# Symmetric attention scores: half of the diagonal chunk of query groups 1 to 4, its place in the program, and a trip through DRAM for its corners

## The chip, the cores and the metric

One core of one Trainium2 chip runs the program. The time is the device time of one execution in microseconds (us). A profiled execution gives the trace that is quoted here; its engines are called PE (TensorE matmuls), PEld (TensorE weight loads), DVE (VectorE), ACT (ScalarE), POOL (GpSimd) and SP (SyncE, which only issues transfers here).

## The reference

```python
scores = (1 / S) * np.matmul(z, z.transpose(0, 2, 1))   # B = 8, S = 3072, 64 wide
attn = np.maximum(scores, 0.0) ** 2
x = u * np.matmul(attn, v)                              # 256 wide
...
x = _moe_ref(x, ...)      # 8 experts, top 1, 256 -> 1024 -> 256
return _moe2_ref(x, ...)  # max of three products, then one more
```

`z` meets itself, so the score matrix of a batch is symmetric, and so is its rectified square.

## The kernel before, in words

The program has three stages: attention over 8 batches, the experts, and a last dense layer. The change is in the first.

A batch's 3072 rows are cut into 6 chunks of 512. A **group** is one batch `b` and one chunk `q` of queries; there are 48, in the order of batches and then of `q` from 0 to 5. A **unit** is one group and one block `kb` of 128 keys; a group has 24 units, four for each chunk `c` of keys. `unit(t)` turns a running number into group, batch, chunk and key block.

fp32 products are made of fp32r parts, a high and a low one. For a unit, `scores(t)` makes a tile `s` of 128 keys x 512 queries with two matmuls of 512 columns (L265 with `hh`, L266 with `ll`; the weights are the key block of `hl`). `square(t, s)` rectifies it on ACT into `a` (L271) and squares it on ACT (L274) or on DVE (L277), whichever is less ahead by a running count of nanoseconds (`hold`, `ahead`). `split_a(t)` makes the high part `ahi` on ACT (L299) and the low part `alo` on DVE (L300). `attend(t)` multiplies them with the values: four times a matmul of 512 columns (L332) and one of 256 (L333).

Symmetry is used between chunks already. For key chunks behind the query chunk (`c > q`) DVE also turns the tile in 32x32 blocks (L306, `turned`), and each finished chunk, 1 MB, is stored to DRAM (`mirror`, L310). When group `c` comes to key chunk `q`, it does not compute: `fetch_back` has read the chunk into a tile `back` (four transfers, L318), and `split_a` reads that. Such units are called **mirrored**; group `q` has 4q of them, at its start. There are three `back` tiles in a ring, so that a fetch waits until the chunk of three fetches ago is used up (`done` in the loop over `pairs`).

The order of the program is written out by hand as a loop over steps `t`. In step `t`, `split_a` is called for unit t+3 (`AH` is 3), `scores` and `square` for unit t+5 unless it is mirrored, and `attend` for unit t. What is scheduled with `at(t, ...)` comes first in its step. `step()` runs pieces of background jobs in between: loading `z` and `v`, the end of a group (`arrive`), the routing for the experts (`route`), and `weights`, which converts the last layer's weights in 48 parts of twelve DVE instructions (`split_m2`, on tiles `wex`, `wsg`, `wmt`, `wrs`, `fr`, `both`). A piece is put off where DVE or ACT is counted too far ahead. What is left of `weights` after the attention is run behind the first block of the experts (`for _ in weights: pass`); there DVE also makes a table of block addresses (`lims`, `tab`), from which SP reads where to fetch the rows of the third block (`wgs<-xb`).

## Time and profile before

| | |
|---|---|
| median of 3 runs | 4076.74 us (4076.67 to 4077.44) |
| the profiled execution, its own time | 4076.14 us |
| its span, first to last instruction | 4074.1 us |
| mean granted TensorE clock, share of full | 0.998 |
| PE busy, PEld busy | 4032.8 us (99%), 3441.0 us (84%) |
| DVE busy, ACT busy, POOL busy | 3151.4 us (77%), 2411.1 us (59%), 1143.9 us (28%) |
| last matmul of the attention starts | 2005.03 us |

The span is what the trace shows; 2 us of the execution's time lie around it. Busy time of PE contains modelled ends of matmuls, so the distance between the starts of matmuls says more than their durations.

### The profile page before, as it was taken

To read this page: it belongs to the slowest core of one execution; us is meant where nothing else is said; L and a number is where in the kernel's file an instruction comes from. 1 tells how busy PE (TensorE), PEld (TensorE's weight loads), DVE (VectorE), ACT (ScalarE), POOL (GpSimd) and SP (SyncE) were. 2 spreads that over 40 slices of the span, in tenths; PEclk is the share of its full clock that TensorE was granted. 3 is DMA by queue.
4 is the path that set the end of the run, shared out by engine and by line. 5 is a ranking of instruction groups with operands and counts; after the bars stand their busy time and mean duration, and the time that the engine had idled before them with its cause. 6 is when DMAs were issued, how large, how long until landed. Compare 5 with 4: busy or idle time off the path is not lost. (4 is left out here: it accounts for less than half of the span.)

```text
span 4074.1 us, 62853 instructions
## 1 busy us (share of the span) xinstructions
PE 4032.8 (99%) x21156; PEld 3441.0 (84%) x21156; DVE 3151.4 (77%) x5925; ACT 2411.1 (59%) x4419; POOL 1143.9 (28%) x1228
## 2 busy tenths in 40 slices
PE   9999999999999999999999999999999999999999
PEld 7888888888888888888899999888888888888887
DVE  8888888888888888888755555677777777777776
ACT  8777787877868778687533333344444444444443
POOL 0111111112111121111321121255455455455453
PEclk9999999999999999999999999999999999999999
DMA  6877868677786777958654554412211221221211
GB/s 179 193 191 194 186 189 196 177 192 175 198 205 164 198 193 195 202 163 196 153 144 129 130 139 121 102 31 32 42 33 31 42 34 29 42 36 27 42 32 21
DMA packets 880303, 507.14 MB, mean 124 GB/s; under 512 B 518050, under 2 KB 831522, under 8 KB 864578
## 3 DMA queue, kind: packets, MB, share of 16 engines
q1 hardware_dynamic: 856946, 438.04, 46.3%
q0 software_dynamic: 20880, 64.28, 5.2%
q8 instruction: 175, 2.87, 0.3%
q14 instruction: 190, 1.56, 0.1%
q10 hardware_dynamic: 2112, 0.39, 0.1%
HBM read 277.62 MB, written 200.31 MB: 117 GB/s over the span
## 5 line engine op out<-in xcount | busy, mean ns | idle before, releaser
L332 PE MATMUL acc<-vt,ahi 128*128 128x512 f32 x4608 | 1647.2, 396 | 4.5 <-DVE x L349 2.4
L333 PE MATMUL acc<-vt,alo 128*128 128x256 f32 x4608 | 1291.4, 280 | 3.9 <-DVE alo L300 3.9
L1253 PE MATMUL ph<-mx,mw 128*128 128x512 f32 x4536 | 1196.9, 395 | 6.3 <-POOL mx L668 3.9
L332 PEld LDWEIGHTS acc<-vt,ahi 128*128 128x128 f32 x4608 | 866.0, 188 | 210.6 <-DVE x L349 4.3
L1253 PEld LDWEIGHTS ph<-mx,mw 128*128 128x128 f32 x4536 | 850.7, 188 | 213.2 <-POOL mx L668 14.1
L333 PEld LDWEIGHTS acc<-vt,alo 128*128 128x128 f32 x4608 | 870.6, 189 | 34.5 <-DVE alo L300 5.4
L1259 ACT ACTIVATE spare<-ph 128x512 f32<-128x512 f32 x648 | 384.6, 597 | 645.2 <-PE ph L1253 641.0
L300 DVE TENSOR_TENSOR alo<-a,ahi 128x512 fp32r<-128x512 f32 x672 | 465.6, 693 | 171.1 <-ACT ahi L299 163.5
L112 POOL DMA_INDIRECT xb<-x,idx x192 | 223.7, 1165 | 1332.4 <-DVE x L349 1058.5
L1290 PE MATMUL y<-fh,mo 128*128 128x512 f32 x1728 | 536.1, 392 | 0.3 <-DVE fh L668 0.3
L271 ACT ACTIVATE a<-s 128x512 f32<-128x512 f32 x672 | 398.6, 593 | 166.9 <-PE s L266 132.4
L668 POOL TENSOR_TENSOR fh<-fc,fh 128x512 fp32r<-128x512 f32 x285 | 367.1, 1295 | 415.2 <-ACT fh L667 399.0
L299 ACT ACTIVATE ahi<-a 128x512 fp32r<-128x512 f32 x672 | 411.6, 618 | 0.9 <-DVE a L277 0.9
L299 ACT ACTIVATE ahi<-back 128x512 fp32r<-128x512 f32 x480 | 291.5, 627 | 165.4 <-PE acc L332 125.9
L1290 PEld LDWEIGHTS y<-fh,mo 128*128 128x128 f32 x1728 | 324.7, 188 | 75.1 <-DVE fh L668 0.6
L300 DVE TENSOR_TENSOR alo<-back,ahi 128x512 fp32r<-128x512 f32 x480 | 328.7, 690 | 38.9 <-ACT ahi L299 28.5
L306 DVE STREAM_TRANSPOSE turned<-a 128x512 f32<-128x512 f32 x480 | 337.7, 704 | 0.0
L274 ACT ACTIVATE a<-a 128x512 f32<-128x512 f32 x496 | 314.0, 633 | 15.8
L694 ACT ACTIVATE h_hi<-ph 128x512 fp32r<-128x512 f32 (+1 forms) x232 | 125.4, 546 | 264.2 <-PE ph L690 235.6
L265 PE MATMUL s<-hh,hl 128*128 128x512 f32 x672 | 269.4, 401 | 9.5 <-DVE hl L201 7.1
L266 PE MATMUL s<-ll,hl 128*128 128x512 f32 x672 | 266.3, 396 | 0.0
L695 DVE SCALAR_TENSOR_TENSOR h_lo<-ph,h_hi 128x512 fp32r<-128x512 f32 (+1 forms) x232 | 144.5, 628 | 156.0 <-ACT h_hi L694 116.8
(169 smaller groups left out, 5321.8 us busy)
## 6 DMA issues: line engine op xcount, KB each, us to landing
mirror<-turned SPq DMA_DIRECT2D x120, 1024.0 KB
back<-mirror SPq DMA_DIRECT2D x480, 256.0 KB
ut<-in_u SPq DMA_DIRECT2D x48, 512.0 KB
out<-xr SPq DMA_DIRECT2D x188, 128.0 KB
vr<-in_v POOLq DMA_DIRECT2D x46, 512.0 KB
xq<-xb SPq DMA_DIRECT2D x320, 64.0 KB
r<-in_moe_w SPq DMA_DIRECT2D x16, 1024.0 KB
wgs<-xb SPq DMA_DIRECT2D x192, 64.0 KB
```

Of the source, the lines that this page charges most:

```text
L265: nc.tensor.matmul(s, w, hh, start=True, stop=False)
L271: nc.scalar.activation(a, s, AF.Relu)
L274: nc.scalar.activation(a, a, AF.Square)
L299: nc.scalar.activation(hi, a, AF.Copy)
L300: nc.vector.tensor_tensor(lo, a, hi.bitcast(F32), op=ALU.subtract)
L306: nc.vector.transpose(out=turned[0][:, :, n], in_=a.rearrange("k (c j) -> k c j", j=Q))
L332: nc.tensor.matmul(o, hn, vv, start=kb == 0, stop=False, skip_group_check=True)
L333: nc.tensor.matmul(o[:, 0], ln, vv[:, 0], start=False, stop=kb == KB - 1, skip_group_check=True)
L668: eng.tensor_tensor(lo, src, hi.bitcast(F32), op=ALU.subtract)
L1253: nc.tensor.matmul(bank[:, 0:e.n], lt[:, s, c], rt[:, m], start=start and k == 0, stop=k == 2, skip_group_check=True)
L1259: nc.scalar.activation(t, bank[:, 0:e.n], AF.Copy)
L1290: nc.tensor.matmul(flat[2 * t + d][:, 0:p.n], mo[f][:, s, d], p.h[g, i, t][m], start=(g, i, k) == (0, 0, 0), stop=(g, i, k) == (NG2 - 1, 1 ...
```

## The change

In groups with `q` from 1 to 4 (`half`) the diagonal key chunk (`c == q`) is moved to the end of the group (`order`) and treated as a mirrored one. Its scores are made earlier, by `diagonal(g, n)`, in steps in which a mirrored unit makes none. Key block n computes only the queries from block n on: 512, 384, 256 and 128 columns for n = 0 to 3. The squares go into a `back` tile. The blocks below the diagonal are turned by DVE in 32x32 blocks into `tips` (3, 2, 1 and 0 transposes), stored to DRAM (`store_corner`, four transfers) and read back into the same tile (`fetch_corner`, three transfers). The `back` ring now serves these tiles as well, so the steps at which chunks are fetched are computed anew.

```diff
@@ -231,10 +231,13 @@
         NG = B * QG
         NU = NG * KB
 
+        half = [0 < q < QG - 1 for q in range(QG)]
+        order = [[c for c in range(QG) if c != q or not half[q]] + [q] * half[q] for q in range(QG)]
+
         def unit(t):
-            g, kb = divmod(t, KB)
+            g, i = divmod(t, KB)
             b, q = divmod(g, QG)
-            return g, b, q, kb
+            return g, b, q, order[q][i // TB] * TB + i % TB
 
         a_t = {}
         back = {}
@@ -243,6 +246,12 @@
             (p, c, q): dpool.tile([P, TB * T], F32, name=f"mirror{p}_{c}_{q}")
             for p in range(2) for q in range(QG) for c in range(q)
         }
+        TX = TB * (TB - 1) // 2 * Q
+        corner = {
+            (p, q): dpool.tile([P, TB * TX], F32, name=f"corner{p}_{q}")
+            for p in range(2) for q in range(QG) if half[q]
+        }
+        tips = {}
         hi_t = {}
         lo_t = {}
         acc = {}
@@ -282,7 +291,57 @@
 
         def mirrored(t):
             _, _, q, kb = unit(t)
-            return kb // TB < q
+            return kb // TB < q or kb // TB == q and half[q]
+
+        def back_tile():
+            back_n[0] += 1
+            return slab("back") if back_n[0] % 3 else back_p.tile([P, TB, TB, P], F32, name="back")
+
+        back_n = [-1]
+
+        def tip_of(n):
+            return slice(n * (n - 1) // 2 * Q, n * (n + 1) // 2 * Q)
+
+        def diagonal(g, n):
+
+            b, q = divmod(g, QG)
+            finish_job(("z", (b, q)))
+            hold("pe", 427 * (TB - n) // TB)
+            hh, ll = zq[g]
+            w, cols = hl[b, q][:, n * P:(n + 1) * P], slice(n * P, T)
+            s, a = bank_tile("s", [P, T]), slab("a")
+            nc.tensor.matmul(s[:, cols], w, hh[:, cols], start=True, stop=False)
+            nc.tensor.matmul(s[:, cols], w, ll[:, cols], start=False, stop=True)
+            nc.scalar.activation(a[:, cols], s[:, cols], AF.Relu)
+            hold("act", 500 * (TB - n) // TB)
+            if n == 0:
+                back[b, q, q] = back_tile()
+                tips[g] = slab("turned", [P, TB, TX], name="tips")
+            x = a[:, cols].rearrange("j (k p i) -> j p k i", p=TB, i=Q)
+            o = back[b, q, q][:, n].rearrange("j p (k i) -> j p k i", i=Q)[:, :, n:]
+            if ahead("act") <= ahead("dve"):
+                nc.scalar.activation(o, x, AF.Square)
+                hold("act", 530 * (TB - n) // TB)
+            else:
+                nc.vector.tensor_tensor(o, x, x, op=ALU.mult)
+                hold("dve", 600 * (TB - n) // TB)
+            for m in range(n + 1, TB):
+                tip = tips[g][:, :, tip_of(m)][:, :, n * Q:(n + 1) * Q]
+                nc.vector.transpose(out=tip, in_=back[b, q, q][:, n, :, m * Q:(m + 1) * Q])
+                hold("dve", 240)
+
+        def store_corner(g):
+            b, q = divmod(g, QG)
+            dst = corner[b % 2, q].rearrange("(p j) (c x) -> p j c x", j=Q, c=TB)
+            for p in range(TB):
+                nc.sync.dma_start(dst[p].rearrange("j c x -> c j x"), tips[g][:, p])
+            tips.pop(g)
+
+        def fetch_corner(g):
+            b, q = divmod(g, QG)
+            src = corner[b % 2, q].rearrange("k (c x) -> k c x", c=TB)
+            for n in range(1, TB):
+                nc.sync.dma_start(back[b, q, q][:, n, :, 0:n * Q], src[:, :, tip_of(n)])
 
         def split_a(t):
             g, b, q, kb = unit(t)
@@ -299,7 +358,7 @@
             nc.scalar.activation(hi, a, AF.Copy)
             nc.vector.tensor_tensor(lo, a, hi.bitcast(F32), op=ALU.subtract)
             hold("act", 520)
-            hold("dve", 600 if c <= q else 1200)
+            hold("dve", 600 if mirrored(t) else 1200)
             if c > q:
                 if n == 0:
                     turned[0] = slab("turned")
@@ -311,8 +370,8 @@
                         mirror[b % 2, q, c], turned[0].rearrange("k c n i -> k (c n i)")
                     )
 
-        def fetch_back(n, b, c, q):
-            back[b, c, q] = t = slab("back") if n % 3 else back_p.tile([P, TB, TB, P], F32, name="back")
+        def fetch_back(b, c, q):
+            back[b, c, q] = t = back_tile()
             src = mirror[b % 2, c, q].rearrange("(p j) (n m x) -> m j n p x", j=Q, m=TB, x=P)
             for m in range(TB):
                 nc.sync.dma_start(t[m * Q:(m + 1) * Q], src[m])
@@ -320,17 +379,18 @@
         def attend(t):
             g, b, q, kb = unit(t)
             hold("pe", 1280)
-            if kb == 0:
+            i = t % KB
+            if i == 0:
                 acc[g] = [None] * TB
             hi, lo = hi_t.pop(t), lo_t.pop(t)
             vv = vt[b, kb // TB][:, kb % TB]
             for n in range(TB):
-                if kb == 0:
+                if i == 0:
                     acc[g][n] = bank_tile("acc", [P, 2, D])
                 o = acc[g][n]
                 hn, ln = hi[:, n * P:(n + 1) * P], lo[:, n * P:(n + 1) * P]
-                nc.tensor.matmul(o, hn, vv, start=kb == 0, stop=False, skip_group_check=True)
-                nc.tensor.matmul(o[:, 0], ln, vv[:, 0], start=False, stop=kb == KB - 1, skip_group_check=True)
+                nc.tensor.matmul(o, hn, vv, start=i == 0, stop=False, skip_group_check=True)
+                nc.tensor.matmul(o[:, 0], ln, vv[:, 0], start=False, stop=i == KB - 1, skip_group_check=True)
 
         xhi = xs_p.tile([P, 2 * TB, D], F32R, name="xhi")
         xlo = xs_p.tile([P, 2 * TB, D], F32R, name="xlo")
@@ -618,13 +678,28 @@
                 at(t0, start, ("v", key), prep_v(*key))
             if b or c:
                 at((b * QG + c) * KB - 12, spread_z, b * QG + c)
-        pairs = [(b, c, q) for b in range(B) for q in range(QG) for c in range(q)]
-        done = []
-        for n, (b, c, q) in enumerate(pairs):
-            t0 = b * G + q * KB + c * TB
-            made = b * G + c * KB + (q + 1) * TB - AH
-            at(max(made, done[n - 3] if n >= 3 else 0, t0 - 24), fetch_back, n, b, c, q)
-            done.append(t0 + TB - AH)
+        done = [-99] * 3
+        taken = -99
+        halved = {}
+        for g in range(NG):
+            b, q = divmod(g, QG)
+            for c in range(q):
+                t0 = g * KB + c * TB
+                made = b * G + c * KB + (order[c].index(q) + 1) * TB - AH
+                assert taken <= max(made, done[-3], t0 - 24)
+                taken = max(made, done[-3], t0 - 24)
+                at(taken, fetch_back, b, c, q)
+                done.append(t0 + TB - AH)
+            if half[q]:
+                t0 = g * KB + max(TB * q - 10 - (q == 2), -AH - 2)
+                assert t0 >= max(taken, done[-3])
+                taken = t0
+                for n in range(TB):
+                    assert mirrored(t0 + n + AH + 2)
+                    halved[t0 + n] = g, n
+                at(t0 + TB, store_corner, g)
+                at(t0 + TB + 2, fetch_corner, g)
+                done.append(g * KB + KB - AH)
         at(KB // 2, load_u, 0)
         for g in range(NG):
             e0 = (g + 1) * KB
@@ -837,6 +912,8 @@
                 ready(t + AH + 2)
                 if not mirrored(t + AH + 2):
                     square(t + AH + 2, scores(t + AH + 2))
+                elif t in halved:
+                    diagonal(*halved.pop(t))
                 step()
             if 0 <= t + 2 < NU:
                 _, b, _, kb = unit(t + 2)
```

Three places in the order of instructions follow, without times. On PE, the first diagonal chunk of the program (batch 0, group 1): before, the first score pair of the chunk, the attend matmuls of one unit (`acc<-vt,...`) and the next pair; then the same of the change.

```order
L265 MATMUL s_737<-hh_527,hl_196 128x512
L266 MATMUL s_737<-ll_528,hl_196 128x512
L332 MATMUL acc_268<-vt_654,ahi_695 128x512
L333 MATMUL acc_268<-vt_654,alo_696 128x256
L332 MATMUL acc_271<-vt_654,ahi_695 128x512
L333 MATMUL acc_271<-vt_654,alo_696 128x256
L332 MATMUL acc_274<-vt_654,ahi_695 128x512
L333 MATMUL acc_274<-vt_654,alo_696 128x256
L332 MATMUL acc_277<-vt_654,ahi_695 128x512
L333 MATMUL acc_277<-vt_654,alo_696 128x256
L265 MATMUL s_772<-hh_527,hl_196 128x512
L266 MATMUL s_772<-ll_528,hl_196 128x512
```

```order
L313 MATMUL s_691<-hh_535,hl_204 128x512
L314 MATMUL s_691<-ll_536,hl_204 128x512
L392 MATMUL acc_276<-vt_516,ahi_622 128x512
L393 MATMUL acc_276<-vt_516,alo_623 128x256
L392 MATMUL acc_279<-vt_516,ahi_622 128x512
L393 MATMUL acc_279<-vt_516,alo_623 128x256
L392 MATMUL acc_282<-vt_516,ahi_622 128x512
L393 MATMUL acc_282<-vt_516,alo_623 128x256
L392 MATMUL acc_285<-vt_516,ahi_622 128x512
L393 MATMUL acc_285<-vt_516,alo_623 128x256
L313 MATMUL s_720<-hh_535,hl_204 128x384
L314 MATMUL s_720<-ll_536,hl_204 128x384
```

The second pair has 384 columns instead of 512, and the pairs stand four attend units earlier than before, between mirrored units.

On DVE, after the first block of the experts (`xr<-y,xr` ends that block; `h_lo<-ph,h_hi` is the low part of a hidden tile that PE multiplies next): before, the address table begins at once.

```order
L723 SCALAR_TENSOR_TENSOR xr<-y,xr 128x256 x4
L891 TENSOR_TENSOR lims<-runs,base 128x8
L892 TENSOR_SCALAR lims<-lims 128x1
L894 CAST tab<-lims 1x8
L896 TENSOR_SCALAR last<-lims 1x8
L898 TENSOR_SCALAR two<-lims 1x8
L904 TENSOR_TENSOR xT<-thr,last 1x8x6
L905 TENSOR_TENSOR xT<-thr,two 1x8x43
L906 TENSOR_SCALAR xT<-two 1x8
L695 SCALAR_TENSOR_TENSOR h_lo<-ph,h_hi 128x512
```

With the change, conversion of the last layer's weights (`wex`, `wsg`, `wmt`, `wrs`, `fr`, `both`) stands there; 22 such instructions come before `lims`.

```order
L798 SCALAR_TENSOR_TENSOR xr<-y,xr 128x256 x4
L547 TENSOR_SCALAR wex<-wex 128x128
L549 TENSOR_SCALAR wsg<-w_24518 128x128
L551 SCALAR_TENSOR_TENSOR wsg<-wex,wsg 128x128
L553 TENSOR_SCALAR wmt<-w_24518 128x128
L555 SCALAR_TENSOR_TENSOR wmt<-w_24518,wmt 128x128
L770 SCALAR_TENSOR_TENSOR h_lo<-ph,h_hi 128x512
L557 TENSOR_TENSOR wmt<-wmt,wsg 128x128
L559 TENSOR_SCALAR wrs<-w_24518 128x128
L743 TENSOR_TENSOR w<-r_24246,w 128x512
L564 SCALAR_TENSOR_TENSOR fr<-wrs,wsg 128x128
L566 TENSOR_TENSOR wmt<-wmt,both 128x128
```

The table is then finished (`tab<-nblk`) right ahead of the transpose `xt<-wgs`, which reads rows that SP fetches by that table; before, 15 instructions stood between the two, now three.

```order
L992 TENSOR_REDUCE nblk<-xT 1x8
L770 SCALAR_TENSOR_TENSOR h_lo<-ph,h_hi 128x512
L993 CAST tab<-nblk 1x8
L103 TENSOR_TENSOR away<-tok_65,lims 128x36
L104 SCALAR_TENSOR_TENSOR own<-away 128x36
L105 SCALAR_TENSOR_TENSOR away<-away,tokN 128x36
L748 STREAM_TRANSPOSE xt<-wgs 128x384
L743 TENSOR_TENSOR xT<-xt,xT 128x384
L770 SCALAR_TENSOR_TENSOR h_lo<-ph,h_hi 128x512
```

On SP, group 4 of batch 0: before, the fetch of a mirrored chunk (`back<-mirror_0_5`) is followed by weight parts and the next fetch.

```order
L318 DMA back<-mirror_3_4_126 32x16x128 x4
L229 DMA ut<-in_u 128x4x256
L318 DMA back<-mirror_0_5_127 32x16x128 x4
L509 DMA mwd_75<-both 256x1x128
L460 DMA w_2500<-in_moe_w 128x256
L318 DMA back<-mirror_1_5_128 32x16x128 x4
L222 DMA hh<-hl 64x512 x2
L222 DMA ll<-hl 64x512 x2
L318 DMA back<-mirror_2_5_129 32x16x128 x4
```

With the change the corner is stored right behind it, and the next fetch (`back<-mirror_1_5`) stands behind the three reads of the corner.

```order
L377 DMA back<-mirror_3_4_126 32x16x128 x4
L229 DMA ut<-in_u 128x4x256
L377 DMA back<-mirror_0_5_127 32x16x128 x4
L337 DMA corner_4_150<-tips 4x32x192 x4
L222 DMA hh<-hl 64x512 x2
L222 DMA ll<-hl 64x512 x2
L344 DMA back<-corner_4_150 128x4x32
L344 DMA back<-corner_4_150 128x4x64
L344 DMA back<-corner_4_150 128x4x96
L377 DMA back<-mirror_1_5_128 32x16x128 x4
L569 DMA mwd_75<-both 256x1x128
L520 DMA w_2678<-in_moe_w 128x256
```

The four issues of the store, the spread of `z` (`hh`, `ll`) and the three reads now stand between two fetches of mirrored chunks.

## Rows read from the trace of the kernel before

**Rows 1.** One window of 250 us; busy us per engine, PEclk, DMA share, GB/s.
```profile
500.00:750.00 250.00, 249.61 (x1389) 215.58 (x1388) 214.39 (x476) 193.81 (x358) 38.60 (x60) 1.00 0.75 188
```

**Rows 2.** The longest waits of PE, 20 to 2000 us; total, times, longest.
```profile
PE acc L332 <- DVE x L349: 2.4, 6, 0.4
PE acc L332 <- ACT ahi L299: 2.2, 2, 1.7
```

**Rows 3.** Timeline of PE; start, us, instruction.
```profile
403.29 0.39 PE L265 MATMUL s<-hh,hl 128*128 128x512 f32 x1
403.52 0.39 PE L266 MATMUL s<-ll,hl 128*128 128x512 f32 x1
403.75 0.28 PE L378 MATMUL pm<-xhi,wgs 128*128 128x256 f32 x1
...
404.70 0.39 PE L332 MATMUL acc<-vt,ahi 128*128 128x512 f32 x1
```

**Rows 4.** Timeline of PE in the experts, 384 columns.
```profile
2052.21 3.29 PE L690 MATMUL ph<-xT,e 128*128 128x384 f32 x18
2055.34 0.40 PE L709 MATMUL y<-e,h_hi 128*128 128x256 f32 x2
```

**Rows 5.** Groups by line and shape, DVE and ACT; busy, mean ns, idle before.
```profile
L277 DVE TENSOR_TENSOR a<-a 128x512 f32<-128x512 f32 x173 | 118.3, 684 | 32.7 <-ACT a L271 26.7 <-issue 4.9
L386 DVE STREAM_TRANSPOSE L<-pm 128x128 f32<-128x128 f32 x1 | 0.3, 307 | 0.0
L300 DVE TENSOR_TENSOR alo<-back,ahi 128x512 fp32r<-128x512 f32 x480 | 328.7, 690 | 38.9 <-ACT ahi L299 28.5 <-issue 4.4 <-PE acc L333 1.1
L274 ACT ACTIVATE a<-a 128x512 f32<-128x512 f32 x494 | 312.7, 633 | 15.8
L299 ACT ACTIVATE ahi<-back 128x512 fp32r<-128x512 f32 x480 | 291.5, 627 | 165.4 <-PE acc L332 125.9 <-issue 17.3 <-DVE alo L300 8.4
```

**Rows 6.** Windows of groups 1 and 4 of batch 2.
```profile
555.20:599.30 44.10, 44.10 (x248) 38.06 (x246) 38.26 (x93) 37.03 (x69) 0.00 (x0) 1.00 0.64 170
...
682.40:719.80 37.40, 37.40 (x210) 32.39 (x209) 32.21 (x72) 23.48 (x44) 12.51 (x20) 1.00 1.06 242
```

**Rows 7.** Weight conversion on DVE, dearest and cheapest of its twelve groups of 48.
```profile
L508 DVE TENSOR_TENSOR both<-wmt,fr 128x128 fp32r<-128x128 f32 x48 | 13.5, 281 | 0.4
...
L487 DVE TENSOR_SCALAR wex<-wex 128x128 int32<-128x128 int32 x48 | 9.5, 198 | 0.3
```

**Rows 8.** Timeline of DVE at the start of the experts; idle time before in brackets.
```profile
2035.93 0.15 DVE L916 CAST tab<-nblk 1x8 int32<-1x8 f32 x1
...
2040.27 0.69 DVE L695 SCALAR_TENSOR_TENSOR h_lo<-ph,h_hi 128x512 fp32r<-128x512 f32 x1 [0.67 <-ACT h_hi L694]
...
2043.09 0.69 DVE L695 SCALAR_TENSOR_TENSOR h_lo<-ph,h_hi 128x512 fp32r<-128x512 f32 x1 [1.46 <-issue]
2043.69 0.57 DVE L673 STREAM_TRANSPOSE xt<-wgs 128x384 f32<-128x384 f32 x1
2044.85 0.56 DVE L668 TENSOR_TENSOR xT<-xt,xT 128x384 fp32r<-128x384 f32 x1 [0.59 <-issue]
2045.97 0.69 DVE L695 SCALAR_TENSOR_TENSOR h_lo<-ph,h_hi 128x512 fp32r<-128x512 f32 x1 [0.56 <-ACT h_hi L694]
```

**Rows 9.** Timeline of SP's issues in the same stretch.
```profile
2039.19 4.11 SPq L127 DMA_DIRECT2D wgs<-xb  x8
```

**Rows 10.** Timeline of PE at the attention's end; idle before in brackets.
```profile
1993.55 0.50 PE L332 MATMUL acc<-vt,ahi 128*128 128x512 f32 x1 [1.67 <-ACT ahi L299]
...
2000.92 0.56 PE L333 MATMUL acc<-vt,alo 128*128 128x256 f32 x1 [3.71 <-DVE alo L300]
```

**Rows 11.** Windows behind these two waits.
```profile
1994.20:1997.50 3.30, 2.93 (x8) 2.13 (x8) 3.30 (x3) 1.44 (x4) 3.27 (x3) 0.50 1.10 279
2000.90:2004.30 3.40, 3.38 (x11) 2.90 (x12) 0.56 (x1) 0.18 (x1) 0.05 (x1) 0.51 0.00 0
```

**Rows 12.** Waits of SP's queue from 400 to 2000 us.
```profile
SPq L318 <- DMA mirror<-turned: 67.2, 18, 5.2
```

2 lines of the change are left out of this document (1 added, 1 removed).

## The prediction

> **What bounds it now.** I read the attention first, in windows of 250 us: PE is busy for 249.6 of 250 us at the full clock, DVE for 214, ACT for 194, and the DMA engines for 0.75 of the time [rows 1]. Since PE's busy time has modelled ends, I then asked for its waits: the largest two from 20 to 2000 us sum to 4.6 us, in a stretch of 1980 us [rows 2]. Last, the starts of its matmuls: two of 512 columns start 0.23 us apart, and eight of 256 take 0.95 us from the first to what follows them, 0.119 each [rows 3]; eighteen of 384 take 3.13, 0.174 each [rows 4]. Cost follows columns, with no idle time between. So PE sets the attention's length, one matmul after the other, and a matmul column taken from it there is time gained, as long as nothing else starts to hold PE up.
>
> **What is removed.** A diagonal chunk had eight matmuls of 512 columns. Now there are two each of 512, 384, 256 and 128. With c for one of 128 columns, a group saves 2 x (3 x 0.23 - 0.174 - 0.119 - c) = 2 x (0.397 - c) us. There are 32 such groups (8 batches, q from 1 to 4). No fp32r matmul of 128 columns is in the trace, so c has bounds: half of a 256-column one, 0.06, gives 0.674 a group and 21.6 us in all; as much as one of 512, 0.23, gives 0.334 and 10.7 us. I take c = 0.119, the price of its nearest neighbour: every matmul here brings a weight load of 128 columns, and nothing in the trace shows such a load in less time than 0.119. That gives 0.556 a group, **17.8 us**.
>
> The Trainium skill bears on this choice: "TensorE: Matmul & The Clock Gate", section "LDWEIGHTS (loading the stationary operand)", says that a load costs its columns over 1.2, in ns, and the next section says that the fast load is not on for FP32. Its 107 ns for 128 columns would make the saving 18.6 us, an estimate from that page; no run so far shows a load that isn't hidden.
>
> **What is added beside it.** DVE gets six transposes of 128x128 elements a group, 0.307 us each by the nearest one [rows 5], 1.84 a group and 59 us in all. But the rule that hands out squares answers to it: in the new order DVE has 85 squares, where there were 176 (72 full ones and 13 in diagonal blocks); 91 fewer at 0.684 [rows 5] give back 62. DVE's sum stays. ACT has those squares now, 58 us at 0.633 [rows 5], and its rectifying and squaring of narrowed tiles saves at most 30 us for each (32 x 768 columns at 0.633 per 512), less for their fixed parts. Without any saving, 58 in 1980 us would be 7 of 250 on top of 194. The densest halved group for DVE is group 1, busy for 38.3 of 44.1 us, and ACT for 37.0 [rows 6]: 44.1 becomes 43.5, and 38.3 plus 1.84, without any square given back, is 40.1. No engine passes PE. The permuted reads cost nothing: mirrored units, read in that pattern already, take 0.690 on DVE and 0.627 on ACT [rows 5]. I put these at zero; the cover is the three units by which `split_a` runs ahead. If it were gone, all of the 1.84 would be on the path.
>
> The corner's transfers are 0.39 MB out and 0.39 MB in, per group; at 188 GB/s [rows 1] that is 4.2 us of all engines in some 41 us, so 0.75 goes to about 0.85. SP gets seven issues more. Also zero, while the corner is there in time (the second rival).
>
> **What is moved.** The background job that converts the last layer's weights is put off more often in the new order. Before, its last part is done within the attention. Now 22 of its DVE instructions stand at the start of the experts, ahead of the address table. By their groups' means, from 0.198 to 0.281 us [rows 7], one part of twelve is 2.89 us, and these 22 are 5.35. In the attention they lay in DVE's free time, which PE never sees. Here they do not: DVE worked without a break after the table, and its idle time ahead of `xt<-wgs` is 0.67 + 1.46 = 2.13 us [rows 8]. So DVE reaches that transpose 3.2 us later, at 2046.9 in the old count, and the table, now only just ahead of it, is complete at about 2046.6 instead of 2036.1 [rows 8]. Behind the table hangs SP: its fetch of the eight pieces began at 2039.19 [rows 9], and the transpose of the first half started at 2043.69 [rows 8], with no wait for a transfer named; 4.5 us is therefore enough from the first issue to the data. If SP may start only with the complete table, the transpose comes at about 2051.6 with half a us to read the address; if an earlier part of the table is enough (written some 2.3 us of DVE work before its end) and the data are quicker, at about 2048. The `h_lo` behind it ended 3.0 us after the transpose's start, at 2046.66 [rows 8]; without PE to wait for, 2.4 us: the low part of the turned tile starts 1.16 after the transpose and takes 0.56, `h_lo` 0.69 [rows 8]. So at 2050.4 to 2054.0. PE wants that tile for the seventh of its eight steps of second products. The next block starts at 2052.21 [rows 4] and a step is twelve products of 0.12, 1.44 us, so it is wanted at 2049.3. PE comes 1.1 to 4.7 us late, and the other half of the rows, behind in the same queue, adds up to 1. A pause can also drop PE's clock: after waits of 1.67 and 3.71 us at the attention's end [rows 10] the granted share was 0.50 for 3.3 us [rows 11], which loses up to 1.7 us. Together 2 to 8 us, and I take **4 us**. (Zero is not excluded, should the transfers be far quicker.)
>
> The chunk fetches move by a few steps. The shortest lead from a fetch's step to its first use is eight units both before and after; before, ACT's time ahead of `ahi<-back` names no transfer [rows 5]. Zero.
>
> The attention's end, with its waits [rows 10], has the same program except for two squares that go from DVE to ACT. ACT and DVE both wait there, so I put it at zero, with 1 us either way.
>
> **Sum.** 4076.14 of the profiled execution (2.0 us of it outside the span) - 17.8 + 4 = 4062.3. The median of the runs shown is 0.6 above the profiled execution, so 4063.
>
> **Rivals.** First: 128 columns cost as much as 512 (a fixed price for short fp32r matmuls). Then 10.7 - 4 = 6.7 us remain, 4070. Nothing in the trace speaks for it; 256 and 384 are in proportion, but none is shorter. Its counterpart, c = 0.06, gives 21.6 - 4, so 4059; for it speaks the same proportion, against it the weight load.
>
> Second, on the other side: in group 4 the corner comes back too late. SP's queue is strict in order: behind the 1 MB fetch of a chunk stand the store, four transfers of `hh` and `ll`, then the reads, which wait for the store to land. Such a wait of a fetch for its own store took 67.2 us in 18 times, 3.7 each and 5.2 at most [rows 12]. In group 4 the DMA share is 1.06 already [rows 6], so transfers queue. From the end of the last transposes to the use by PE there are eleven units: a unit's attend matmuls take 4 x (0.23 + 0.119) = 1.40 us, with full scores 1.86; four units have scores, so 17.2 us. Against it: four issues (2.6), the wait (5.2), three issues (1.9) and as long a landing (5.2) make 15, with the 1 MB ahead (4.3 us at 242 GB/s) just 19 if nothing overlaps. Since issuing overlaps with the transfers ahead, I expect it to fit, but closely. The point where it decides: 13.8 us of net gain over 8 such groups is 1.7 us of wait each. With 3 us of wait and 1.7 of clock each it costs 38 and gives 4101; with the other 24 groups in it, more.
>
> The Trainium skill, "DMA: Bandwidth & Descriptors", section "Specifications", speaks against the change here too: below 512 B a transfer misses line rate, and the corner's reads are runs of 128 to 384 B. No row of this trace parts such reads from others.
>
> Third: the moved conversion hides after all, or costs more. Within the 2 to 8 us, and part of the forecast's own range.
>
> **Chances.** The forecast, from 4060 to 4067, 0.50; c = 0.06, 4056 to 4060, 0.17; c = 0.23, 4067 to 4074, 0.18; the late corner, from small waits to 4101, 0.15. The range leaves the late corner out, and starts at the lower bound of c with an attention's end 1 us better (4076.7 - 21.6 - 1 = 4054) and ends at its upper bound with the dear end of the move (4076.7 - 10.7 + 8 = 4074). 0.2%, about what a measurement of this kernel tells from no change, is 8.2 us, so faster means under 4068.6 and slower over 4084.9. The first two cases are faster, and a few hundredths of the third; most of the third, and the small waits of the fourth, are the same. Faster 0.70, same 0.18, slower 0.12.
>
> **What would show it.** In the profile after: matmuls `s<-hh,hl` of 128 columns, whose distance to the next start is c; the attention's last matmul at 2005 - 17.8 = 1987 us; no new wait of PE in the attention (a wait of ACT or DVE for `back<-corner` in group 4 with PE idle behind it is the late corner); DVE's busy share in the attention unchanged; and at the experts' start DVE waiting for `wgs`, PE waiting for `h_lo`, 2 to 8 us. The forecast is wrong if PE has waits in groups 1 to 4, if c is not near 0.12, or if the table's delay reaches past that one block.

## The result, and the profile after

The changed kernel takes 4132.19 us (median of 4 runs) beside 4077.09 for the kernel before on the same chip: ratio 1.0138, 95% interval 1.0126 to 1.015. It is slower by 55 us, where I forecast 14 us faster. The profiled execution took 4132.7 us, its span 4130.6, so 56.5 us more than before; 52.7 of these lie ahead of the attention's last unit, whose first matmul starts at 2055.85 instead of 2003.20.

The columns were saved as planned, and more cheaply than I had taken them. The timeline of PE in the kernel after, around a pair of matmuls of 128 columns:

```profile
868.88 0.28 PE L393 MATMUL acc<-vt,alo 128*128 128x256 f32 x1
869.00 0.22 PE L313 MATMUL s<-hh,hl 128*128 128x128 f32 x1
869.06 0.27 PE L314 MATMUL s<-ll,hl 128*128 128x128 f32 x1
869.17 0.44 PE L392 MATMUL acc<-vt,ahi 128*128 128x512 f32 x1
```

From start to start that is 0.06 and 0.11, and so it is in all 32 such pairs (medians 0.061 and 0.112). But PE, whose two largest waits were 4.6 us in all in this stretch [rows 2], has 52.5 us of them now. The waits of PE in the kernel after, 20 to 2000 us (total, times, longest):

```profile
PE pm L438 <- DVE xlo L430: 28.7, 12, 4.5
PE acc L392 <- DVE x L409: 22.1, 17, 3.8
PE acc L392 <- ACT ahi L358: 1.7, 2, 1.3
```

To place the loss I took the distance between the first attend matmuls of neighbouring units, after less before, and the mean over batches 1 to 6. Apart from the units whose scores went or came, the time is lost at a few places: the first unit of group 0 (+0.96 us), the seventh of group 1 (+1.62), the first of group 2 (+1.06), and in group 5 the first three (+1.82), the seventh to ninth (+4.41) and two more (+0.43). That is 10.3 us a batch; two thirds of it in group 5, which the change does not touch. These means hide two kinds of batch. Batches 1, 2, 4 and 6 lose 5.8 to 7.2 us at the seventh to ninth unit of group 5 and under 0.8 at the first three; batches 0, 3, 5 and 7 lose 3.9 to 7.3 at the first three, where PE waits for DVE's `x<-acc`, and nearly nothing later. Batch 2, which is shown from here on, is of the first kind.

The windows of batch 2's six groups follow. The columns are the stretch, its length, the busy us of PE, PEld, DVE, ACT and POOL, then the granted clock, the DMA share and GB/s, as in [rows 6], which has groups 1 and 4 of before:

```profile
523.70:568.60 44.90, 44.45 (x242) 38.04 (x241) 39.46 (x71) 42.34 (x84) 10.35 (x18) 1.00 0.58 190
568.60:613.50 44.90, 43.52 (x248) 37.56 (x246) 37.55 (x90) 34.82 (x66) 0.00 (x0) 1.00 0.71 192
613.50:654.20 40.70, 39.28 (x218) 33.82 (x218) 35.62 (x83) 30.89 (x60) 10.63 (x18) 1.00 0.86 237
654.20:694.80 40.60, 40.60 (x237) 35.50 (x236) 33.61 (x91) 29.53 (x58) 0.25 (x1) 1.00 0.74 181
694.80:731.50 36.70, 36.70 (x210) 31.93 (x209) 30.01 (x70) 23.49 (x48) 11.28 (x20) 1.00 0.91 207
731.50:779.40 47.90, 43.41 (x233) 37.49 (x232) 33.26 (x78) 29.74 (x55) 3.00 (x4) 0.93 0.82 170
```

In group 4, the fifth line, the DMA engines have a share of 0.91 and move 207 GB/s, where it was 1.06 and 242 before [rows 6]. Before, group 5 was 40.20 us long, with PE busy throughout and the transfers at 0.68:

```profile
719.80:760.00 40.20, 40.20 (x232) 35.14 (x231) 34.00 (x79) 29.80 (x57) 5.79 (x8) 1.00 0.68 144
```

Group 5 can be read step by step. First SP's queue in the kernel after (start, us of issuing):

```profile
710.77 3.71 SPq L337 DMA_DIRECT2D corner<-tips  x4
...
718.75 1.19 SPq L222 DMA_DIRECT2D ll<-hl  x2
723.15 1.92 SPq L344 DMA_DIRECT2D back<-corner  x3
725.11 0.62 SPq L520 DMA_DIRECT2D w<-in_moe_w  x1
725.83 2.66 SPq L377 DMA_DIRECT2D back<-mirror  x4
...
733.68 9.01 SPq L377 DMA_DIRECT2D back<-mirror  x8
```

Between 719.94 and 723.15 SP stands at the read of the corner until its store has landed. The fetch of group 5's second chunk, behind it, leaves at 725.83, that of its third at 733.68, together with the fourth. On ACT, the waits that end with these transfers (in brackets the idle time before):

```profile
725.45 0.63 ACT L358 ACTIVATE ahi<-back 128x512 fp32r<-128x512 f32 x1 [4.51 <-DMA back<-corner]
...
743.88 1.15 ACT L358 ACTIVATE ahi<-back 128x512 fp32r<-128x512 f32 x2 [4.89 <-DMA back<-mirror]
```

DVE stands behind ACT, and on DVE the second half of `xlo`, a piece of the router's work, stands behind the late unit's `alo`. PE wants that `xlo` at once, and waits in order, although the unit that it attends next was split already at 739.7. DVE and then PE in the kernel after:

```profile
744.54 0.69 DVE L359 TENSOR_TENSOR alo<-back,ahi 128x512 fp32r<-128x512 f32 x1 [4.23 <-ACT ahi L358]
745.15 0.70 DVE L190 STREAM_TRANSPOSE pz<-zn 64x512 f32<-64x512 f32 x1
745.78 0.64 DVE L430 TENSOR_TENSOR xlo<-xT,xhi 128x512 fp32r<-128x512 f32 x1
```

```profile
746.47 0.58 PE L438 MATMUL pm<-xlo,wgs 128*128 128x256 f32 x1 [4.08 <-DVE xlo L430]
```

For the 6 us behind that wait the granted clock is 0.53, nearly all of it at the lower of the two levels, 1.2 GHz. PE is busy throughout, so the 4.08 cost some 6 x 0.47 = 2.8 us more; the distances of the units give 6.8 for this batch:

```profile
746.50:752.50 6.00, 6.00 (x24) 5.61 (x25) 3.71 (x6) 2.19 (x6) 0.75 (x1) 0.53 1.19 195
```

### The profile page after: what moved, and what is told of

Its sections match the earlier page's. It is cut to its first block, busy times and chain, and to the rows that moved or that the text cites. A ratio compares the mean times of both kernels' runs of the same rounds, so it can differ in the third digit from the quotient of the medians.

```text
span 4130.6 us, 63363 instructions
## 1 busy us (share of the span) xinstructions
PE 4034.3 (98%) x21156; PEld 3442.0 (83%) x21156; DVE 3126.1 (76%) x6026; ACT 2411.1 (58%) x4510; POOL 1139.9 (28%) x1228
## 5 line engine op out<-in xcount | busy, mean ns | idle before, releaser
L112 POOL DMA_INDIRECT xb<-x,idx x192 | 214.8, 1119 | 1335.5 <-DVE x L409 617.9
L358 ACT ACTIVATE ahi<-back 128x512 fp32r<-128x512 f32 x608 | 371.2, 625 | 265.2 <-PE acc L392 131.6
L359 DVE TENSOR_TENSOR alo<-back,ahi 128x512 fp32r<-128x512 f32 x608 | 418.1, 691 | 132.1 <-ACT ahi L358 121.4
L359 DVE TENSOR_TENSOR alo<-a,ahi 128x512 fp32r<-128x512 f32 x544 | 375.7, 691 | 144.1 <-ACT ahi L358 137.7
L280 ACT ACTIVATE a<-s 128x512 f32<-128x512 f32 x544 | 320.5, 589 | 109.2 <-PE s L275 98.2
L358 ACT ACTIVATE ahi<-a 128x512 fp32r<-128x512 f32 x544 | 332.7, 617 | 0.7 <-DVE a L286 0.7
L283 ACT ACTIVATE a<-a 128x512 f32<-128x512 f32 x472 | 298.7, 633 | 15.0
L1343 DVE TENSOR_TENSOR fc<-ph,spare 128x512 f32<-128x512 f32 x216 | 148.6, 688 | 135.2 <-PE ph L1330 70.0
L1347 DVE TENSOR_TENSOR fc<-fc,xq 128x512 f32<-128x512 f32 x216 | 237.3, 1099 | 7.4
```

What stands on the lines that cost most here:

```text
L280: nc.scalar.activation(a, s, AF.Relu)
L283: nc.scalar.activation(a, a, AF.Square)
L358: nc.scalar.activation(hi, a, AF.Copy)
L359: nc.vector.tensor_tensor(lo, a, hi.bitcast(F32), op=ALU.subtract)
L1347: nc.vector.tensor_tensor(acc2[key], acc2[key], t, op=MAX)
```

## The experiments

Fourteen kernels, all edits made to the changed kernel. My theories: A, the diagonal's tile sits in the ring of three that the fetched chunks use, until the group's last unit, so group 5's third chunk is fetched late; B, the corner itself is late and holds SP; C, background pieces are put off and then forced out in lumps at the turns of groups. D to G came up on the way. The rounds ran on different chips; the kernel before had medians of 4075.7 to 4077.1 us in them, so one or two us between two rounds say nothing.

The table has the us lost per batch at each place (means of batches 1 to 6, from the starts as above: group and units counted from 0), and the time against before.

```
                                g0:0  g1:6  g2:0 g4:20+ g5:0+ g5:6+ g5:15+ ratio (95%)
changed kernel                  0.96  1.62  1.06  0.29  1.82  4.41  0.43   1.0138 (1.0126-1.0150)
1 ring                          0.73  1.63  1.05  2.11  2.04 -0.07  0.00   1.0108 (1.0091-1.0125)
2 without group 4               0.73  1.62  1.10  0.00  0.22 -0.03  0.00   1.0032 (1.0020-1.0045)
3 corner on POOL                0.81  1.62  1.05  3.65  0.57  0.01  0.00   1.0086 (1.0069-1.0103)
4 gate                          1.24 -0.03 -0.10  0.47  2.71  3.93  0.01   1.0088 (1.0071-1.0105)
5 ring, early                   0.73  1.62  1.06  1.05  6.15 -0.07  0.00   1.0155 (1.0138-1.0172)
6 ring, early, gate             1.35 -0.04 -0.11  0.10  6.93  0.12  0.62   1.0097 (1.0080-1.0113)
7 order only                    0.73  1.63 -0.28  0.02  0.03 -0.03  0.00   1.0035 (1.0023-1.0048)
8 as 6, loads two ahead         1.95 -0.03 -0.11  0.10  0.08  0.74  2.19   1.0045 (1.0031-1.0060)
9 as 5, loads two ahead         1.32  1.62  1.09  0.10  0.08  0.20  1.81   1.0062 (1.0046-1.0079)
10 no group 4, gate, charge     0.00 -0.03 -0.09  0.00  0.39 -0.02  0.00   0.9958 (0.9945-0.9972)
11 as 8, charge                 0.53 -0.03 -0.09  0.10  0.08  0.59  2.35   1.0001 (0.9992-1.0010)
12 as 11, no trip in group 4    0.00 -0.03 -0.05  0.10  0.08 -0.06  0.00   0.9959 (0.9944-0.9974)
13 as 11, its corner on POOL    0.10 -0.03 -0.09  1.42  1.16 -0.06  0.00   0.9981 (0.9972-0.9991)
14 as 12, the store back        0.51 -0.03 -0.09  0.10  0.08 -0.06  1.20   0.9977 (0.9967-0.9987)
```

**1. Ring.** In group 4 the diagonal's tile comes from the ring of turned tiles, and no longer counts for the fetches:

```diff
-                back[b, q, q] = back_tile()
+                back[b, q, q] = slab("turned", [P, TB, TB, P], name="diag") if q == QG - 2 else back_tile()
...
-                done.append(g * KB + KB - AH)
+                if q < QG - 2:
+                    done.append(g * KB + KB - AH)
```

> Group 4's diagonal block stands in a buffer of the ring of turned tiles (which group 4 hardly uses), not in the ring of three for fetched chunks; so chunks 1 and 2 of group 5 are fetched some eight units earlier. Theory A (the diagonal's buffer, held to the group's last unit, delays those fetches): the waits of PE at units 6 and 7 of group 5, 4.4 us a batch, go, and most of the 1.8 at units 0 and 1: 35 to 50 us less than the changed kernel, 4082 to 4097 us. Theory B (the corner itself is late, with SP held by its store and its reads): units 0 and 1 stay as they are, ACT still waits for the corner, and the time stays above 4110 us.

4120.73 us. The wait at the seventh unit of group 5 is gone, so A is right about that place, but the time is higher than A gave: the second chunk's fetch now stands ahead of the corner, and the corner's reads leave at 30 to 32 us from the start of group 4 in batches 1 to 6, where they left at 27 to 30. ACT's waits in this kernel:

```profile
ACT ahi L358 <- DMA diag<-corner: 45.7, 18, 7.7
```

The changed kernel had 32.1 us of such waits, and 45.6 for `back<-mirror`, which are 6.9 here. B holds too: what was taken from the one went in part to the other.

**2. Without group 4.**

```diff
-        half = [0 < q < QG - 1 for q in range(QG)]
+        half = [0 < q < QG - 2 for q in range(QG)]
```

> Only groups 1 to 3 are halved; group 4 is as in the kernel before. If all that group 5 lost (6.2 us a batch, some 49) comes from group 4's halving, by whichever of theories A and B, and the 0.68 us a batch saved there is given up, the time is 4132 - 49 + 5 = 4088 us, and what is lost at groups 0, 1 and 2 (3.6 us a batch) stays. If those losses are an after-effect of group 5's late buffers too, it is about 4060 us. If group 5 loses its time by DVE's added work of all groups, nothing changes: 4130 us.

4089.58 us, 1.6 from the first case. Group 4's halving makes all but 0.2 us of what group 5 loses; groups 0 to 2 lose theirs without it (0.96 becomes 0.73 in group 0).

**3. Corner on POOL.**

```diff
-                nc.sync.dma_start(dst[p].rearrange("j c x -> c j x"), tips[g][:, p])
+                nc.gpsimd.dma_start(dst[p].rearrange("j c x -> c j x"), tips[g][:, p])
...
-                nc.sync.dma_start(back[b, q, q][:, n, :, 0:n * Q], src[:, :, tip_of(n)])
+                nc.gpsimd.dma_start(back[b, q, q][:, n, :, 0:n * Q], src[:, :, tip_of(n)])
```

> The corner's stores and reads are issued by POOL, everything else as in the changed kernel, so SP is never held by a corner's store. Theory B (SP held): the chunks of group 5 leave earlier and PE's waits in group 5 mostly go, 4085 to 4100 us. Theory A (the buffer of the third chunk comes free only with the diagonal's last unit): the fetch of chunk 2 still stands behind that read; at most the chunk-1 fetch is earlier, and the time stays at 4115 to 4135 us.

4111.72 us, between B's range and what A allows at best. Group 5 is nearly clean although the ring is as in the changed kernel, and the end of group 4 loses 3.65. The ring alone is therefore not the cause either: the earlier fetches of run 1 and the freed queue of this run each take away the 4.41. In each of the two another transfer is late instead, here the corner, for which ACT waits 65.9 us.

**4. Gate.**

```diff
-            if clock[0] < clock[1] or KB < clock[0] < 3 * (NU - KB) and (ahead("dve") > 2000 or ahead("act") > 3000):
+            if clock[0] < clock[1] or KB < clock[0] < 3 * (NU - KB) and (ahead("dve") > 3000 or ahead("act") > 3000):
```

> The rule that puts off background pieces while DVE has more than 2.0 us of work ahead is set to 3.0; so 2 pieces of routing are forced out in a lump at the start of group 2, not 8, and none at the start of group 0. Theory C (those lumps cost the 1.06, 0.96 and perhaps 1.62 us at the starts of groups 2, 0 and in group 1): 8 to 29 us less than the changed kernel, 4103 to 4124 us. Rival: the lumps are covered and the losses there come from buffers and transfers: within 5 us of 4132.

4112.43 us, 19.8 less, of which some 3.5 lie behind the attention (see the conversion below). C holds for groups 1 and 2: they lose nothing now. It does not touch group 5, and makes group 0's first unit worse.

**5 and 6. Ring and an early corner, then with the gate.** Scores of group 4's diagonal at steps 0 to 3 of the group, where they stood at 6 to 9; store and read move with them.

```diff
-                t0 = g * KB + max(TB * q - 10 - (q == 2), -AH - 2)
+                t0 = g * KB + (0 if q == QG - 2 else max(TB * q - 10 - (q == 2), -AH - 2))
```

> As the first experiment (group 4's diagonal in the ring of turned tiles), and its scores six program steps earlier, so that the corner is asked for 11 steps before its use, not 5. Theory A+B (group 4 and 5 lose time to two lateness in one queue: the chunk behind the diagonal's buffer, and the corner itself): the 2.0 us a batch at the end of group 4 and the 2.0 at the start of group 5 that the first experiment left go; some 30 us less than its 4120.7, 4085 to 4095 us. Rival: the rest comes from DVE's added transposes and routing pieces at that boundary; then it stays at 4112 to 4125 us.

> The experiment before and the rule for background pieces at 3.0 us together. If theories A+B and C each hold by themselves, their gains add: 4090 - 20 = 4070 us (4062 to 4076), the first version faster than the kernel before, with the saved columns (2.6 us a batch) showing. If the one was only hidden by the other, it stays over 4080 us.

4139.05 and 4115.10 us. The first is above both of its cases, and the second fell to the case over 4080. In the fifth kernel ACT waits only 8.6 us in all for chunks and corner, yet its group 5 loses 6.15 at the first units. DVE in it, at that turn in batch 4:

```profile
1247.03 0.69 DVE L359 TENSOR_TENSOR alo<-back,ahi 128x512 fp32r<-128x512 f32 x1 [0.20 <-ACT ahi L358]
1255.42 0.23 DVE L543 TENSOR_SCALAR wex<-w 128x128 int32<-128x128 int32 x1 [7.70 <-DMA w<-in_moe_w]
1255.63 1.42 DVE L409 SCALAR_TENSOR_TENSOR x<-acc,x 128x256 f32<-128x256 f32 x4
```

The first instruction of a background part of the weight conversion stands on DVE ahead of `x<-acc`, which empties the banks that PE waits for, 6.5 us here. Its load was issued at 1249.31, behind chunk fetches and `hh`, `ll`. SP's queue in the same kernel:

```profile
1243.42 3.91 SPq L377 DMA_DIRECT2D back<-mirror  x4
1247.55 1.73 SPq L569 DMA_DIRECT2D mwd<-both  x1
1249.31 0.61 SPq L520 DMA_DIRECT2D w<-in_moe_w  x1
```

So DVE catches up early, takes the next part, and runs into its load. That is theory D. The changed kernel has the same in batches 0, 5 and 7, where DVE stands 2.7 to 4.7 us at such a load ahead of `x<-acc`.

**7. Order only.** The diagonal last, with full scores at their usual place:

```diff
-        half = [0 < q < QG - 1 for q in range(QG)]
+        half = [0] * QG
+        last = [0 < q < QG - 1 for q in range(QG)]
...
-        order = [[c for c in range(QG) if c != q or not half[q]] + [q] * half[q] for q in range(QG)]
+        order = [[c for c in range(QG) if c != q or not last[q]] + [q] * last[q] for q in range(QG)]
```

> The kernel of the change with only its new order: in groups 1 to 4 the diagonal chunk is attended last, but its scores are full ones at their usual place, and there is no corner. If the order by itself moves the group's end work into lumps (6 and 2 pieces of routing are forced out at the starts of groups 2 and 4, against 4 and 1), it costs 1 to 2 us a batch: 4083 to 4093 us. If the losses at groups 1 and 2 come from the halved scores alone (six transposes on DVE, less time of PE for them), it is within 5 us of before, 4072 to 4082 us.

4089.47 us, in the first range. The losses at groups 0 and 1 (0.73 and 1.63) come with the order and the planner's numbers, which this run doesn't part: the charge of experiments 10 and 11 is 1.2 us here for all six diagonal chunks. The loss at group 2 and all of group 5's come with the halved scores and the corner.

**8 and 9. Weight loads two ahead.** In the versions of 6 and 5 (the space for the third buffer comes from letting `fr` share `rs`):

```diff
-            ahead = load_m2(*parts[0])
+            ahead = [load_m2(*part) for part in parts[:2]]
...
-                if i + 1 < len(parts):
-                    ahead = load_m2(*parts[i + 1])
+                if i + 2 < len(parts):
+                    ahead.append(load_m2(*parts[i + 2]))
```

> The version with ring, early corner and gate, and the loads of the background weight parts issued two parts ahead, not one (a third buffer; the space comes from letting the fraction's tile share that of the rest). Theory D (with the corner out of the way, two whole weight parts are worked at the end of group 4, DVE stands in order behind a load that SP issued late, 31.6 + 17.2 us in 7 waits, and PE then waits for DVE at unit 0 of group 5): those waits go, with 5 to 6 us a batch: 4115 - 45 = 4070 us (4062 to 4078). Rival: the load is late however early it is asked for, since SP itself stands behind chunk fetches: 4100 us or more.

> The same without the gate: ring, early corner, and weight loads two parts ahead. Theory D: 4139 - 50 = 4090 us (4082 to 4096), 20 us above the version with the gate, as the gate gave by itself. If the weights' load is not what holds DVE at group 5's start, it stays over 4120 us.

4093.45 and 4101.92 us. D is right about the place: the loss at group 5's start falls from 6.9 and 6.2 to 0.1. Each is 12 to 23 us above what I gave, since about 2 us a batch appear at the sixteenth unit of group 5, where ACT stands ahead of the fifth chunk's first unit (6.5 us in batch 2 of the eighth kernel).

**10 and 11. The planner's charge.** The change had altered what the planner charges DVE for the low part of a unit: 1.2 us, the price with a turning, also for the diagonal chunks of groups 0 and 5, which turn nothing. Set back:

```diff
-            hold("dve", 600 if mirrored(t) else 1200)
+            hold("dve", 600 if c <= q else 1200)
```

The tenth has this, the gate, and groups 1 to 3 alone; the eleventh is the eighth with it.

> Groups 1 to 3 halved (group 4 as before the change), the gate at 3.0 us, and one line set back: the planner's charge for a unit's low part is 0.6 us again for the diagonal chunks of groups 0 and 5, which turn nothing (the change charged them 1.2, so squares went to ACT and routing pieces were put off at the turn from group 5 to group 0). If the losses are separate: 4089.6 - 21 (gate, as in its own run) - 4 (conversion back in the attention) - 6 (0.7 us a batch at group 0's first unit) = 4059 us, 4054 to 4066, faster than the kernel before. If they only take each other's place: 4075 us or more.

> The version with ring, early corner, gate and weight loads two parts ahead (4093.5), with the charge set back as well. Theory F (the charge makes the 1.95 us a batch at group 0's first unit): 4093.5 - 15.6 = 4078 us, 4073 to 4084, and no wait of PE for x at group 0. Rival (ACT is late there by the halved group 1's own work): 4093 us.

4059.92 us (ratio 0.9958, 0.9945 to 0.9972), the best of all, and 4078.02, as expected. The charge made most of group 0's loss, 1.95 in the eighth and 0.53 in the eleventh: it sent squares to ACT, which then came late to `x<-acc`. ACT and then DVE in the sixth kernel, which has the charge, at the turn to batch 5:

```profile
1282.59 0.63 ACT L283 ACTIVATE a<-a 128x512 f32<-128x512 f32 x1
1283.12 0.61 ACT L194 ACTIVATE hl<-pz 64x512 fp32r<-64x512 f32 x1
1283.64 1.16 ACT L408 ACTIVATE x<-acc 128x256 f32<-128x256 f32 x4
```

```profile
1284.03 1.42 DVE L409 SCALAR_TENSOR_TENSOR x<-acc,x 128x256 f32<-128x256 f32 x4 [1.76 <-ACT a L283]
```

In the kernel before, DVE made two squares ahead of its `x<-acc` at this turn, and PE had no wait. The 0.53 left in the eleventh is gone in the twelfth, without group 4's trip, and back in the fourteenth with the store alone; by what way was not followed. No run has the gate in the kernel before; PE's waits there are some 5 us in all, so at most that much of the tenth's gain of 17 us could be the gate's alone. PE's waits in the tenth, 20 to 2000 us:

```profile
PE acc L393 <- DVE alo L359: 5.2, 2, 5.0
PE acc L392 <- DVE x L409: 3.5, 8, 1.7
PE pm L438 <- DVE xlo L430: 0.7, 1, 0.7
```

**12. No trip in group 4.** The eleventh, with full scores for group 4's diagonal at the early place, and no store or read of its corner. DVE's six transposes stay.

```diff
+            n0 = 0 if q == QG - 2 else n
-            w, cols = hl[b, q][:, n * P:(n + 1) * P], slice(n * P, T)
+            w, cols = hl[b, q][:, n * P:(n + 1) * P], slice(n0 * P, T)
...
-                at(t0 + TB, store_corner, g)
-                at(t0 + TB + 2, fetch_corner, g)
+                if q < QG - 2:
+                    at(t0 + TB, store_corner, g)
+                    at(t0 + TB + 2, fetch_corner, g)
```

> As the one before, but in group 4 the diagonal's scores are full ones, at the place of the halved ones, so its corner isn't stored nor read (the six transposes on DVE stay, and nothing reads them): 0.39 MB out and 0.39 MB in less per batch, 0.7 us of PE more. Theory E (the transfers fill all engines from the middle of group 4 on, share 1.0 to 1.2, and the corner's are what makes the later chunks of group 5 late, 3.1 us a batch): 4078 - 25 + 5 = 4058 us, 4053 to 4066. If instead the order and the place of the diagonal make them late, or DVE's transposes: 4078 + 5 = 4083 us.

4060.36 us, 17.7 less, although group 4's columns are not saved (0.59 us a group, 4.7 in all): the trip costs 22.4 us. (In the attention alone the profiled execution is 22.2 us shorter, so the trip costs 26.9 there; what lies behind the attention is 3.4 longer, for a reason that no run shows.) Groups 4 and 5 of batch 2 in the eleventh kernel, then in the twelfth:

```profile
688.20:724.70 36.50, 36.50 (x208) 31.75 (x207) 30.33 (x71) 24.46 (x48) 10.51 (x18) 1.00 1.10 228
724.70:768.90 44.20, 41.27 (x232) 35.09 (x231) 32.98 (x77) 28.41 (x55) 5.31 (x7) 1.00 0.82 177
```

```profile
677.60:714.60 37.00, 37.00 (x207) 31.94 (x206) 30.17 (x71) 25.53 (x48) 10.95 (x18) 1.00 1.15 258
714.60:754.90 40.30, 40.30 (x232) 35.10 (x231) 33.96 (x79) 29.80 (x57) 5.80 (x8) 1.00 0.69 145
```

In group 4 the DMA engines are busy nearly all the time in both. With the corner they move 8.3 MB there (228 x 36.5), 0.8 of it the corner, without it 9.5 (258 x 37.0); the rest goes over into group 5, whose chunks are then late. Batches 1 to 6 agree: 224 to 233 GB/s with it, 250 to 259 without.

**13 and 14. Which part of the trip.** The eleventh with group 4's corner issued by POOL (the edit of 3, for `q == QG - 2` alone), and the twelfth with the store back on SP and no read.

> The version with ring, early corner, gate, loads two ahead and charge (4078.0), with the corner of group 4 alone issued by POOL. Theory G (SP's queue, which is never free from the corner's store to the middle of group 5, is what is late): 4060.4 - 5.4 for the columns saved in group 4 = 4055 us, 4052 to 4062. Theory E (the engines are full, and 0.79 MB is 3 to 4 us of them whoever issues it): 4070 to 4082 us.

> The version without a trip in group 4 (4060.4; full scores there), with the corner's store back on SP and still no read, so nothing waits for the store and nothing uses it. Theory G, by the wait: SP loses four issues and no wait, 4060 to 4063 us. Theory E: half of the traffic is back, so about half of the 23 us (17.6 and the 5.4 of the columns): 4068 to 4074 us.

4068.87 and 4065.64 us, neither at the value of one theory. With the issues off SP the chunks are in time: ACT's waits for `back<-mirror`, 36.9 us in the eleventh, are 1.2. But the corner is late. ACT's waits in the thirteenth:

```profile
ACT ahi L358 <- DMA diag<-corner: 43.0, 15, 7.3
ACT vt L211 <- DMA vr<-in_v: 6.5, 5, 2.0
```

Of the trip's 22.4 us, 9.2 go with the issues off SP (of the attention's 26.9, 12.9), so at least that much is the price of having them in SP's queue. The rest is the late corner, and that need not be the traffic, as theory E has it. The corner's blocks are ready 5.7 us after group 4's start in batches 0 to 6 of both kernels. SP stores them at 5.7 to 7.8 in the eleventh, POOL only at 12.2 to 15.2 in the thirteenth, behind its own gathers of rows, one of which waits for an earlier one to land. In batch 2 group 4 starts at 688.2 in the eleventh and at 682.9 in the thirteenth; SP in the eleventh, then POOL in the thirteenth:

```profile
693.88 4.82 SPq L337 DMA_DIRECT2D corner<-tips  x4
```

```profile
692.45 1.28 POOL L112 DMA_INDIRECT xb<-x,idx  x1 [6.03 <-DMA xb<-x,idx]
...
698.13 2.89 POOL L337 DMA_DIRECT2D corner<-tips  x4
```

So POOL's own queue makes the corner later by up to 9.5 us, and how the trip's price divides between the queue and the traffic stays open. The store alone, with no wait behind it, costs 5.3 us (ten runs from 4061.4 to 4072.8, beside four from 4059.5 to 4060.6): four issues and half of the bytes, which this run doesn't part either.

## Why the prediction was wrong, step by step

*What bounds it:* right; with the new waits gone, PE sets the length again and the saving shows (10 and 12).

*The saved columns:* the mechanism was right, the size at its upper bound. In the tenth kernel groups 0 to 3 of a batch are 1.34 - 0.83 - 1.82 - 0.71 = -2.02 us, so 0.67 for each of three halved groups, where I took 0.556 and gave 0.674 for c = 0.06. Over 32 groups that would be 21.5 us instead of 17.8. The starts give a little less: the first matmul of 128 columns takes 0.061 and the second 0.112, so 0.62 a group and 19.9 in all; what makes the 0.05 between the two is not shown. Beside it I set the Trainium skill, "TensorE: Matmul & The Clock Gate", section "LDWEIGHTS (loading the stationary operand)", whose formula comes to 107 ns for a load of 128 columns, an estimate from that page. Taking that length as the least distance between two starts was my step, not the page's, and it failed at the first of each pair, 0.061; the trace has these loads at 0.19 us each, lying over one another.

*Additions on DVE and ACT, zero:* their sums came out as counted. DVE has 72 + 13 = 85 squares, and the six transposes take 0.282 each, not 0.307. What failed is the step from sums to order. I named the three units of lead as cover, and did not ask what the planner does with its own numbers: it put off router and conversion pieces and forced them out where PE waits for them. The gate's run gives 19.8 us for that, some 3.5 of them the conversion's below; the charge's pair (8 and 11) gives 15.4, of which 10.9 lie in the attention.

*The corner's traffic, zero while it is in time:* not zero in group 4, though it was the order of the queue and not full engines that showed in the changed kernel. My own row had a share of 1.06 there [rows 6], so I should have asked what would leave later. In the changed kernel the share of group 4 is 0.91 and the rate 207 GB/s for 242: SP stood still, and what it had not sent came in group 5 (170 GB/s for 144). With the corner early, as in the eleventh kernel, the engines do stay full through group 4 (1.06 to 1.11).

*The chunk fetches, "the shortest lead … is eight units both before and after … Zero":* this is the step that failed most. The minimum is the same, but it is held by other fetches. Group 5's first and second chunk were asked for 16 steps ahead and are now at 12, its third at 16 and now at 8, the second and third behind the corner in the same queue; the two of eight steps that were there before follow them. Eight steps are not too few by themselves: the third chunk of group 3 went from 16 to 8 and that of group 4 from 20 to 8, and nothing beyond the moved scores is lost at either. In group 5 the corner had held SP and used up ACT's lead of three units first; that this is why eight were too few there is my reading of the trace. The runs show the size: without group 4's halving (2) the kernel is 42.6 us faster, and the 4.41 a batch at these chunks goes both with the old leads (1) and with the corner off SP (3).

*The late corner (second rival):* its mechanism was there and it was near the truth in sign, but I let PE wait for the corner itself in group 4. There it loses 0.29 us a batch. The price falls one group later, on the chunks behind it in the queue, 6.7 us a batch, and the sum of 4101 was too small for it.

*The conversion, 4 us:* borne out, though not in all parts. From the attention's last unit to the end the kernel after loses 56.5 - 52.7 = 3.8 us. SP issues the rows from 2098.36 on, just ahead of the table's last instruction, which ends at 2098.8; DVE and PE there:

```profile
2098.66 0.15 DVE L993 CAST tab<-nblk 1x8 int32<-1x8 f32 x1
...
2102.02 0.58 DVE L748 STREAM_TRANSPOSE xt<-wgs 128x384 f32<-128x384 f32 x1 [2.65 <-DMA wgs<-xb]
```

```profile
2103.69 0.50 PE L784 MATMUL y<-e,h_hi 128*128 128x256 f32 x2 [0.50 <-ACT h_hi L769]
2104.42 0.39 PE L784 MATMUL y<-e,h_lo 128*128 128x256 f32 x1 [0.22 <-DVE h_lo L770]
```

DVE waits for `wgs` and PE for `h_lo`, as foretold; from this block's first products to the next block's it is 24.6 us, where it was 22.5, so 2.1 of the 3.8 lie here. With the conversion back in the attention (4) the loss from there to the end is 0.3. In the tenth kernel it is 2.2 all the same, with a clock of 0.68 over the 10 us at the branch behind these blocks (0.85 before); what makes that difference stays open.

*The attention's end, zero:* the tenth kernel's last group is 1.3 us shorter than before; in the changed kernel it can't be told from group 5's other waits.

## What to carry to other kernels

Where one queue issues everything, the shortest lead says little: list, for each transfer, its lead before and after and what stands ahead of it in the queue, and look a group further than the change. A share over the whole run says little about the one group where an added transfer falls: here three halved groups, with the gate and the charge set back, gain 17 us, and the best version with the fourth halved as well, on SP, gave all of it back. When a change touches what a planner is told, follow what the planner will put off, and where it is then forced out; and when waits are removed one at a time, expect the next one to show, as in runs 1, 5 and 8.

## What the runs showed of the hardware

Two fp32r matmuls of 128 columns, each with its own load of the same 128 columns of weights, started 0.061 us (to the second) and 0.112 us (to what follows) apart, medians of 32 pairs; the loads are recorded at 0.19 us each. A PE wait of 4.08 us was followed by 6 us at a granted clock of 0.53, nearly all at the lower of the two levels, with transfers and other engines at work. On SP, four transfers of a chunk took 2.6 to 2.7 us to issue where nothing held them, and up to 7.7 in group 4 of the twelfth kernel, where the engines were full.

With the DMA engines full, group 4 moved 250 to 259 GB/s at shares of 1.12 to 1.15 without the corner (12), 224 to 233 at 1.06 to 1.11 with it (11), and 224 to 232 at 1.05 to 1.10 with its store alone (14). What the Trainium skill says in "DMA: Bandwidth & Descriptors", section "Specifications", that a transfer needs 512 B for line rate, can't be read off this: the store's runs are of 768 B, only the reads' are of 128 to 384 B, and the rate is as low without the reads.
